# Whole weight tiles for the last three pairs, eight chunks with outputs of their own, other planner constants, and a last output tile in two halves

## The chip, the core and the metric

The kernel runs on one core of a Trainium2 chip. Its engines are TensorE (PE, with weight loads shown apart as PEld), VectorE (DVE), ScalarE (ACT), GpSimd (POOL) and SyncE (SP), which here only issues DMAs. The metric is the device time of one execution in microseconds, the median of several.

## The reference

A gated linear attention (a state of 48 by 48 per head that decays by alpha at each step) is followed by a feed-forward layer. 4 batches, 8 heads, 768 steps, head size 48; then 3072 tokens of width 384, hidden width 2048.

```python
state = alpha[t, :, None] * state + k[t] (outer) v[t]     # per batch and head
y[t] = q[t] @ state
h = x @ w_in                                              # x: y as [3072, 384]
g = where(h >= 1, h, where(h <= -1, 0, (h + 1) ** 2 / 4))
out = g @ w_out
```

## The kernel before

**Attention.** The steps are cut into 24 chunks of 128 steps, 6 for each batch. For a chunk, `prepare` loads alpha, k, q and v, makes running products of alpha on VectorE (two scans, lines 546 and 572) and scales q and k by them (lines 586 and 592). Chunks 0 to 6 (`EARLY`) arrive by step and are transposed on PE first (line 485), so that their scans read PSUM; later chunks arrive by head dimension and their scans read SBUF. `attend` then multiplies on PE: keys transposed (line 613), `scores` (628), `update` of the state (641) and `outputs` (768). For chunks below `MERGE` the output product follows in a PE operation of its own once the masks (714) are done; from the chunk after `MERGE` on, one PE operation (`burst`) does the update and scores of chunk j and the outputs of chunk j - 1. `end_chunk` splits the result into a high and a low part in fp32r (lines 792 on ACT, 797 on DVE) and puts it into `ring`.

**Feed-forward.** Chunks form 8 groups of 3 (384 tokens). For each group the 16 blocks f of the hidden width are taken in turn: `hidden` multiplies ring by w_in (line 864, 9 matmuls for the three products of high and low parts), then clips (DVE 908), squares (ACT 893), takes the larger (DVE 919), rounds to fp32r (ACT 923) and subtracts to get the low part (line 924, GpSimd; the very last on DVE). `second` multiplies the result gh by w_out (line 942, 9 matmuls) into three PSUM banks. Two banks hold hidden products, three buffers each hold gf and gh. Groups 0 and 1 share the first half of the weights, then the second half, with their partial sums parked in DRAM. After the last block of a group the three output tiles are copied from PSUM (ACT, or DVE where the planner finds it earlier) and sent out by SP (lines 988 to 1007).

**Weights.** They come as float64: 8 pairs u (blocks 2u and 2u + 1), each with a tile of w_in and one of w_out, 128 x 768 eight-byte words. `decode` turns a tile into a high and a low fp32r part: two ACT conversions (364, 372), two DVE bit operations (380, 391), an integer addition (404), an ACT rounding (417) and a subtraction (419). The addition and the subtraction run on GpSimd, or on DVE where the planner finds that earlier. `PIECES = 2` cuts each of these two into halves of 384 columns, for all pairs.

**The order.** All of it is written as operations with a cost in us, a key and their dependences (`plan.op`), and `Plan.order` simulates the engines in program build: on each engine it takes, among the operations that could begin soonest, the one of the lowest key, and the kernel emits its instructions in the resulting order. Keys count in blocks of the feed-forward. The key of a chunk is its due time, spread over the group before, less a margin (`MARGIN0` for group 0, `MARGIN1` for group 1, `MARGIN` for the rest); that of a weight pair's decode is the first block that needs it less `DECODE` (pair 0: `DECODE0`), and `LAG` more for w_out:

```python
due = since + (begin[n] - since) * (j - first[n] + 1) / groups[n] - (MARGIN, MARGIN0, MARGIN1)[n + 1 if n < 2 else 0]
ready = key - (DECODE if u else DECODE0)
```

Pairs 5, 6 and 7 are first needed at blocks 18, 20 and 22. Where an operation has a second engine (`other`), it stands there with a key higher by `LATER`. Operations marked `port` on DVE and GpSimd are planned one after the other, never at once. PSUM banks of the attention are limited to three at a time, for the first two chunks (`ROOM`) to `FIRST`. Where the plan leaves PE idle early on, it puts in filling matmuls (line 1013). After the plan come a few checks on the running products (lines 1043 to 1058) and the read of a flag (1062).

Of the kernel before, what the change touches and what calls it, by code (L numbers as in the profile page):

```python
# [37 lines left out]
MARGIN0 = 9.0  # L38
MARGIN1 = 6.0
FETCH0 = 18.0  # L40
DECODE0 = 4.0
AHEAD = 15.0
FIRST = 4
ROOM = 2
LATER = 4.0
MERGE = 6
WARMTH = 165.0
PIECES = 2
QHELP = 1
# [183 lines left out]
def gated_attention_ffn(ctx: ExitStack, tc: tile.TileContext, q, k, v, alpha, laid, out):  # L233
    nc = tc.nc
# [76 lines left out]
    with ExitStack() as main:  # L311
# [14 lines left out]
        def buf(where, name, shape, bufs, dtype=F32):  # L326
            plan.pool(name, bufs)
            return Buf(name, lambda: pools[where].tile(shape, dtype, name=name, bufs=bufs))
# [16 lines left out]
        def decode(u, which, raw, parts, key):  # L345

            n = NW * DM

            cols = [slice(i * n // PIECES, (i + 1) * n // PIECES) for i in range(PIECES)]
            part = lambda a: parts().rearrange(PARTS[which])[:, a * n : (a + 1) * n]  # L350
            w = raw
            data = lambda: raw()
            if wide:
# [49 lines left out]
                for c in cols:  # L403
                    add = lambda e, c=c: e.tensor_tensor(  # L404
                        out=bits()[:, c], in0=bits()[:, c], in1=word(I32, 0)[:, c], op=ALU.add
                    )
                    plan.op(
                        "POOL",
                        0.04 + 1.78 / PIECES,
                        key,  # L410
                        lambda add=add: add(nc.gpsimd),
                        [w, raw, (u, which)],
                        [w],
                        port=True,
                        other=("DVE", 0.2 + 1.4 / PIECES, lambda add=add: add(nc.vector), True),
                    )
            plan.op("ACT", 0.8, key, lambda: nc.scalar.copy(out=part(0), in_=data()), [w], [parts])  # L417
            for c in cols:
# [4 lines left out]
                    "POOL",  # L423
                    0.04 + 1.78 / PIECES,
                    key,
# [3 lines left out]
                    port=True,  # L429
                    other=("DVE", 0.08 + 0.8 / PIECES, lambda sub=sub: sub(nc.vector), True),  # L430
                )
# [419 lines left out]
        def hidden(n, f, key, c0=0, c1=GROUP):  # L851
# [73 lines left out]
            ends = (n, f) == (NG - 1, NF - 1)  # L925
            ways = [("POOL", 0.07 + 0.9 * w, lambda: sub(nc.gpsimd), True), ("DVE", 0.08 + 0.45 * w, lambda: sub(nc.vector), True)]
            (e, us, emit, port), other = reversed(ways) if ends else ways
# [5 lines left out]
        def second(seg, f, gh, key, c0=0, c1=GROUP):  # L933
# [30 lines left out]
            for t in ts:  # L964
                ps, ot = o_ps[seg][t], buf("fw", "ot", [P, DM], GROUP)
                place = ("sums", n, t)
                if f0 > 0:
# [274 lines left out]
```

## Time and profile before

| | us |
|---|---|
| median of 3 runs | 521.48 (521.29 to 549.84) |
| the profiled execution | 522.73 |
| its span, first to last instruction | 521.0 |
| PE, DVE, ACT, POOL busy | 502.7, 355.5, 262.3, 269.4 |
| mean granted clock of PE | 0.991 |

The span is what all rows below count from; the profiled execution's own time is 1.73 us more. A row of a timeline gives start and length, the engine, the line of the kernel, output and inputs with their shape, and in brackets how long the engine was idle before it and what released it.

### The profile page before, as it was taken

How to read it: one execution, taken by the hardware profiler on the slowest of the kernel's cores; microseconds unless marked ns; L12 is line 12 of the kernel's file. 1: busy time of each engine (PE TensorE's matmuls, PEld its weight loads, DVE VectorE, ACT ScalarE, POOL GpSimd, SP SyncE). 2: the span in 40 equal slices, each digit the busy share in tenths (PEclk: the TensorE clock that was granted, in tenths of full speed). 3: DMA queues.
4: the chain of work that ended last, by engine and by line, in shares of the span. 5: the costliest groups of instructions: out<-in, count | busy, mean ns of one | idle time of the engine just before them, and what ended most of it. 6: DMA issues, size and time to landing. Idle time of an engine off the chain costs nothing.

```text
span 521.0 us, 12291 instructions
## 1 busy us (share of the span) xinstructions
PE 502.7 (97%) x4874; PEld 484.3 (93%) x4874; DVE 355.5 (68%) x674; ACT 262.3 (50%) x506; POOL 269.4 (52%) x300
## 2 busy tenths in 40 slices
PE   8899899979899999999999999999999999999995
PEld 6788789969899999999999999999999999999995
DVE  6899999877877757578567767478467785343333
ACT  2789997564734444444444443444444444333331
POOL 3678898999954354354354244353354242333330
PEclk9999999998999999999999999999999999999998
DMA  8997968013034323133123422133102200100001
GB/s 239 357 317 235 318 212 311 11 58 120 23 120 122 111 77 80 57 82 123 55 62 79 122 62 77 53 88 123 57 21 59 67 2 8 18 23 23 0 1 50
DMA packets 27902, 52.46 MB, mean 101 GB/s; under 512 B 3808, under 2 KB 13504, under 8 KB 27840
## 3 DMA queue, kind: packets, MB, share of 16 engines
q1 hardware_dynamic: 27840, 51.62, 32.2%
q8 instruction: 40, 0.66, 0.6%
q14 instruction: 22, 0.18, 0.1%
HBM read 43.65 MB, written 5.90 MB: 95 GB/s over the span
## 4 chain that ended last, share of the span: by engine, by line
PE 74%; DVE 9%; DMA 7%; POOL 5%; issue 2%; ACT 1%; SPq 0%; DVEq 0%; POOLq 0%; ACTq 0%
PE ps L942 33%; PE ps L864 32%; DMA wt<-in_laid_w_out 5%; PE ps L768 4%; PE ps L641 2%; POOL wt L419 2%; PE ps L628 2%; POOL gh L924 2%; PE ps L613 1%; DVE w L391 1%; POOL w L404 1%; DVE w L380 1%; DMA raw<-in_laid_tok_q 1%; DVE gf L908 1%; DVE Q L546 1%
## 5 line engine op out<-in xcount | busy, mean ns | idle before, releaser
L942 PE MATMUL ps<-wt,gh 128*128 128x384 f32 x1152 | 226.7, 342 | 5.1 <-POOL gh L924 3.0
L924 POOL TENSOR_TENSOR gh<-gf,gh 128x384 fp32r<-128x384 f32 (+1 forms) x127 | 143.3, 1133 | 162.5 <-ACT gh L923 114.1
L864 PE MATMUL ps<-ring,wt 128*128 128x384 f32 (+1 forms) x1170 | 223.7, 338 | 0.0
L942 PEld LDWEIGHTS ps<-wt,gh 128*128 128x128 f32 x1152 | 202.0, 189 | 7.7 <-POOL gh L924 4.1
L864 PEld LDWEIGHTS ps<-ring,wt 128*128 128x128 f32 x1170 | 204.9, 189 | 0.7 <-DVE ring L797 0.2
L893 ACT ACTIVATE gf<-gf,half_b 128x384 f32<-128x384 f32 x122 | 74.6, 616 | 112.2 <-DVE gf L908 109.3
L908 DVE TENSOR_SCALAR gf<-ps 128x384 f32<-128x384 f32 x122 | 67.0, 552 | 72.4 <-PE ps L864 63.7
L919 DVE TENSOR_TENSOR gf<-gf,ps 128x384 f32<-128x384 f32 (+1 forms) x130 | 70.4, 543 | 50.0 <-ACT gf L893 49.4
L923 ACT CAST gh<-gf 128x384 fp32r<-128x384 f32 (+1 forms) x130 | 65.9, 508 | 71.8 <-DVE gf L919 66.1
L419 POOL TENSOR_TENSOR wt<-w,wt 128x384 fp32r<-128x384 f32 x32 | 39.2, 1245 | 3.4 <-ACT wt L417 3.2
L404 POOL TENSOR_TENSOR w<-w,wt 128x384 int32<-128x384 int32 x30 | 31.0, 1047 | 5.3 <-DVE w L391 2.4
L572 DVE TENSOR_TENSOR_SCAN inv<-raw,bwd 128x511 f32<-128x511 f32 x17 | 33.2, 1954 | 0.0
L546 DVE TENSOR_TENSOR_SCAN Q<-raw,fwd 128x512 f32<-128x512 f32 x17 | 24.0, 1413 | 7.3 <-PE ps L768 7.2
L768 PE MATMUL ps<-Q,both 128*64 128x64 f32 x372 | 26.9, 225 | 1.6 <-issue 1.6
L745 POOL TENSOR_TENSOR state<-state,last 128x192 f32<-128x192 f32 x20 | 12.0, 598 | 30.9 <-DVE state L670 30.9
L768 PEld LDWEIGHTS ps<-Q,both 128*64 128x64 f32 x372 | 23.6, 137 | 4.3 <-issue 2.5
L660 ACT COPY both<-state 48x192 f32<-48x192 f32 x66 | 23.1, 349 | 8.3 <-POOL state L745 6.6
L616 ACT COPY ks<-ps 128x512 f32<-128x512 f32 x24 | 14.1, 586 | 25.9 <-PE ps L613 25.9
L768 PE MATMUL ps<-other,both 128*64 128x64 f32 x372 | 26.7, 225 | 0.0
L592 POOL TENSOR_TENSOR Q<-Q,raw 128x512 f32<-128x512 f32 x18 | 24.1, 1337 | 3.4 <-DVE inv L564 2.0
L714 DVE TENSOR_TENSOR Q<-ps,mask 64x256 f32<-64x256 f32 x48 | 20.3, 423 | 7.5 <-ACT other L678 6.3
L768 PEld LDWEIGHTS ps<-other,both 128*64 128x64 f32 x372 | 23.5, 138 | 0.0
(78 smaller groups left out, 422.6 us busy)
## 6 DMA issues: line engine op xcount, KB each, us to landing
both<-in_laid_v_both SPq DMA_DIRECT2D x48, 128.0 KB, 3.0
wt<-in_laid_w_in SPq DMA_DIRECT2D x8, 768.0 KB, 7.5
wt<-in_laid_w_out SPq DMA_DIRECT2D x8, 768.0 KB, 8.1
vt<-in_laid_v SPq DMA_DIRECT2D x24, 192.0 KB, 2.9
out<-ot SPq DMA_DIRECT2D x24, 192.0 KB, 2.5
raw<-in_laid_dim_a SPq DMA_DIRECT2D x17, 256.0 KB, 2.9
raw<-in_laid_dim_k SPq DMA_DIRECT2D x17, 256.0 KB, 2.9
raw<-in_laid_dim_q SPq DMA_DIRECT2D x17, 256.0 KB, 2.6
```

Of the source, the lines that this page charges most:

```text
L404: add = lambda e, c=c: e.tensor_tensor(out=bits()[:, c], in0=bits()[:, c], in1=word(I32, 0)[:, c], op=ALU.add)
L419: sub = lambda e, c=c: e.tensor_tensor(out=part(1)[:, c], in0=data()[:, c], in1=part(0).bitcast(F32)[:, c], op=ALU.subtract)
L546: lambda: nc.vector.tensor_tensor_scan(flat(Q()), aT(), flat(fwd), 0.0, ALU.mult, ALU.max),
L572: lambda: nc.vector.tensor_tensor_scan(flat(inv())[:, 0:n][:, ::-1], aT()[:, 1 : n + 1][:, ::-1], flat(bwd)[:, 0:n][:, ::-1], bwd[:, G - 1 ...
L768: nc.tensor.matmul(out=ps()[halves[r], to, halves[u]], lhsT=lhsT[:, r, u], rhs=x()[:, g, halves[u]], start=m + u == 0, stop=True, skip_gro ...
L864: nc.tensor.matmul(out=h(), lhsT=win(f, w)[:, kt], rhs=ring[:, at, kt, a, :], start=(m == 0), stop=(m == 3 * KT - 1),)
L893: lambda: nc.scalar.activation(out=gf(), in_=in_(), func=func, scale=scale, bias=bias),
L908: lambda: nc.vector.tensor_scalar(out=gf(), in0=h(), scalar1=-1.0, scalar2=1.0, op0=ALU.max, op1=ALU.min),
L919: lambda: nc.vector.tensor_tensor(out=gf(), in0=gf(), in1=h(), op=ALU.max),
L923: plan.op("ACT", 0.08 + 0.41 * w, key + 0.4, lambda: nc.scalar.copy(out=gh()[:, 0], in_=gf()), [gf], [gh])
L924: sub = lambda e: e.tensor_tensor(out=gh()[:, 1], in0=gf(), in1=gh()[:, 0].bitcast(F32), op=ALU.subtract)
L942: nc.tensor.matmul(out=o_ps[seg][t](), lhsT=gh()[:, a, (t - c0) * CH : (t - c0 + 1) * CH], rhs=wout(f, w), start=(f == f0 and i == 0), sto ...
```

## The change

- `decode` cuts the addition and the subtraction into two only for pairs below `HALVES` = 5; pairs 5, 6 and 7 do each as one instruction of 768 columns. Their planned costs go from 0.93 (a half) to 1.015, and 1.83 for a whole one.
- The planned cost of line 924 on GpSimd goes from 0.97 to 1.00 for 384 columns.
- `MERGE` goes from 6 to 8: chunks 0 to 7 have their outputs in an operation of their own, and the first joined operation is that of chunk 9 with the outputs of chunk 8.
- `DECODE0` goes from 4 to 10, `MARGIN1` from 6 to 5, `FIRST` from 4 to 7.
- The last output tile is copied in two halves of 192 columns, one on ACT and one on DVE; ACT's half is sent from ACT's queue, DVE's from SP's.

```diff
-MARGIN1 = 6.0
+MARGIN1 = 5.0
-DECODE0 = 4.0
+DECODE0 = 10.0
-FIRST = 4
+FIRST = 7
-MERGE = 6
+MERGE = 8
-PIECES = 2
+HALVES = 5
...
-            cols = [slice(i * n // PIECES, (i + 1) * n // PIECES) for i in range(PIECES)]
+            pieces = 2 if u < HALVES else 1
+            cols = [slice(i * n // pieces, (i + 1) * n // pieces) for i in range(pieces)]
...
                         "POOL",
-                        0.04 + 1.78 / PIECES,
+                        0.2 + 1.63 / pieces,
...
-                        other=("DVE", 0.2 + 1.4 / PIECES, lambda add=add: add(nc.vector), True),
+                        other=("DVE", 0.2 + 1.4 / pieces, lambda add=add: add(nc.vector), True),
...
                     "POOL",
-                    0.04 + 1.78 / PIECES,
+                    0.2 + 1.63 / pieces,
...
-                    other=("DVE", 0.08 + 0.8 / PIECES, lambda sub=sub: sub(nc.vector), True),
+                    other=("DVE", 0.08 + 0.8 / pieces, lambda sub=sub: sub(nc.vector), True),
...
-            ways = [("POOL", 0.07 + 0.9 * w, lambda: sub(nc.gpsimd), True), ("DVE", 0.08 + 0.45 * w, lambda: sub(nc.vector), True)]
+            ways = [("POOL", 0.1 + 0.9 * w, lambda: sub(nc.gpsimd), True), ("DVE", 0.08 + 0.45 * w, lambda: sub(nc.vector), True)]
...
                 ps, ot = o_ps[seg][t], buf("fw", "ot", [P, DM], GROUP)
+                r0 = (first[n] + t) * CH
+                if seg == segs[-1] and f0 == 0 and t == ts[-1]:
+                    for e, copied, c in (("ACT", 0.3, slice(0, DM // 2)), ("DVE", 0.33, slice(DM // 2, DM))):
+                        o = plan.op(
+                            e, copied, key, lambda e=e, c=c, ps=ps, ot=ot: copy(e, ot()[:, c], ps()[:, c]), [ps], [ot],
+                            beside=e == "DVE",
+                        )
+                        q_ = {"ACT": ("ACT", nc.scalar), "DVE": ("SP", nc.sync)}[e]
+                        plan.op(
+                            q_[0],
+                            Plan.ISSUE,
+                            key + 1,
+                            lambda q_=q_, c=c, r0=r0, ot=ot: q_[1].dma_start(out=out[r0 : r0 + CH, c], in_=ot()[:, c]),
+                            [],
+                            [],
+                            moved=P * DM * 2,
+                            after=[o],
+                        )
+                    continue
```

## Rows read from the trace of the kernel before

**Rows 1.** The page: busy us, share of the span, instructions.
```profile
PE 502.7 (97%) x4874; PEld 484.3 (93%) x4874; DVE 355.5 (68%) x674; ACT 262.3 (50%) x506; POOL 269.4 (52%) x300
```
**Rows 2.** Windows: stretch, its length, busy us by engine, clock, DMA share, GB/s.
```profile
20.00:70.00 50.00, 45.44 (x658) 39.70 (x657) 47.71 (x95) 44.87 (x90) 42.24 (x54) 1.00 0.88 282
90.00:141.00 51.00, 46.02 (x413) 44.15 (x411) 39.69 (x61) 30.03 (x52) 50.66 (x44) 0.93 0.16 49
141.00:500.00 359.00, 359.00 (x3289) 352.14 (x3289) 228.38 (x446) 156.38 (x309) 147.16 (x163) 1.00 0.23 65
```
**Rows 3.** Timeline of PE around its idle time between 110 and 137 us.
```profile
112.27 0.61 PE L942 MATMUL ps<-wt,gh 128*128 128x384 f32 x2 [0.33 <-ACT gh L923]
115.88 2.61 PE L942 MATMUL ps<-wt,gh 128*128 128x384 f32 x7 [3.00 <-POOL gh L924]
...
136.60 1.66 PE L942 MATMUL ps<-wt,gh 128*128 128x384 f32 x8 [1.66 <-POOL wt L419]
```
**Rows 4.** Windows behind that idle time.
```profile
116.00:122.00 6.00, 6.00 (x19) 6.00 (x20) 5.94 (x8) 2.54 (x5) 5.83 (x5) 0.50 0.39 142
137.00:141.00 4.00, 4.00 (x108) 3.61 (x106) 3.18 (x8) 3.54 (x7) 4.00 (x5) 1.00 0.02 4
```
**Rows 5.** The chain that ended last: start, us, what (113 to 137 us).
```profile
113.86 1.01 POOL w L404
...
134.84 1.72 POOL wt L419
```
**Rows 6.** Timelines of ACT and of POOL ahead of the gap of 3 us.
```profile
111.70 0.51 ACT L923 CAST gh<-gf 128x384 fp32r<-128x384 f32 x1 [0.15 <-DVE gf L919]
...
110.35 3.55 POOL L419 TENSOR_TENSOR wt<-w,wt 128x384 fp32r<-128x384 f32 x2 [0.17 <-ACT wt L417]
...
114.83 0.99 POOL L924 TENSOR_TENSOR gh<-gf,gh 128x384 fp32r<-128x384 f32 x1
```
**Rows 7.** Single lines: durations in ns min/median/max; last row: busy us, mean ns.
```profile
L404 DVE CUSTOM_DVE_ANT_0 w<-wt,w x2: 880/893/906, 91.8 to 136.1; 128x768 uint16<-128x768 uint16 x2
...
L419 POOL TENSOR_TENSOR wt<-w,wt x32: 996/1026/1947, 24.1 to 140.7; 128x384 fp32r<-128x384 f32 x32
...
L924 POOL TENSOR_TENSOR gh<-gf,gh 128x128 fp32r<-128x128 f32 x1 | 0.5, 458 | 0.1
```
**Rows 8.** Groups of instructions between 90 and 141 us: busy us, mean ns, idle before.
```profile
L419 POOL TENSOR_TENSOR wt<-w,wt 128x384 fp32r<-128x384 f32 x16 | 22.0, 1396 | 0.2 <-ACT wt L417 0.2
L924 POOL TENSOR_TENSOR gh<-gf,gh 128x384 fp32r<-128x384 f32 x12 | 15.0, 1247 | 0.0
L919 DVE TENSOR_TENSOR gf<-gf,ps 128x384 f32<-128x384 f32 x13 | 7.1, 549 | 8.3 <-ACT gf L893 8.3
```
**Rows 9.** Timeline of PE: outputs of chunk 5 alone, and of chunk 6 joined.
```profile
63.58 0.30 PE L768 MATMUL ps<-Q,both 128*64 128x64 f32 x2 [0.26 <-issue]
...
101.15 0.27 PE L768 MATMUL ps<-Q,both 128*64 128x64 f32 x1
```
**Rows 10.** The end: chain, SP's issues, a window, landing (us), a half-width copy (ns).
```profile
515.28 0.56 DVE ot L340
...
515.34 1.02 SPq L1001 DMA_DIRECT2D out<-ot  x1
...
516.46 0.38 SPq L1001 DMA_DIRECT2D out<-ot  x1
...
517.00:518.00 1.00, 0.00 (x0) 0.00 (x0) 0.00 (x0) 0.00 (x0) 0.00 (x0) 0.96 0.93 342
...
out<-ot SPq DMA_DIRECT2D x24, 192.0 KB, 2.5
...
L668 DVE COPY state<-ps x4: 357/358/358, 14.0 to 334.4; 128x192 f32<-128x192 f32 x4
```
**Rows 11.** The second scan, from SBUF and from PSUM: ns min/median/max.
```profile
L572 DVE TENSOR_TENSOR_SCAN inv<-raw,bwd x17: 1336/2072/2660, 81.9 to 417.4; 128x511 f32<-128x511 f32 x17
L572 DVE TENSOR_TENSOR_SCAN inv<-ps,bwd x7: 1270/1272/1272, 7.2 to 67.2; 128x511 f32<-128x511 f32 x7
```

## The prediction

> **What bounds the kernel now.** I read the busy times first: TensorE (PE) is busy for 502.7 of 521.0 us, VectorE 355.5, GpSimd 269.4 [rows 1]. A share of the whole span hides stages, so the table by stage comes next [rows 2]. From 141 to 500 us PE is busy 359.00 of 359.00 us at full clock: a step that only moves helper work there gives nothing. From 20 to 70 us VectorE is the fullest engine (47.71 of 50, ScalarE 44.87). From 90 to 141 us it is GpSimd: 50.66 of 51, while PE has 46.02 and a granted clock of 0.93. PE is idle for 4.6 us from 20 to 70, 5.0 us from 90 to 141 and 5.8 us at the end, after its last product, whose copy begins at 515.28 [rows 10].
>
> The timeline of PE shows where the 5.0 us lie [rows 3]: 0.33 us and 3.00 us inside one second product at 112.27 us, released by the GpSimd subtraction that makes the low half of gh (line 924), and 1.66 us at 136.60 us, released by line 419, the last step of a weight tile's decode. The 3 us gap has a second price. From 116 to 122 us the granted clock reads 0.50, the lower of the two levels (1.2 GHz) [rows 4], so those 6.1 us of products are worth half: about 3.1 us more. The 1.66 us gap has no such tail: the clock is 1.00 from 137 us on. Together PE loses 3.33 + 3.1 + 1.66 = 8.1 us between 112 and 137 us.
>
> The chain of waits says who sets this: from 113.86 to 136.56 us it is mostly GpSimd, lines 404, 924 and 419 in turn, and then PE [rows 5]. GpSimd's own timeline shows the gap being made [rows 6]: two halves of line 419 take 3.55 us, a half of line 404 another 1.01, and only then, at 114.83, comes the gh that PE has waited for since 112.9 and whose input ScalarE had ready at 112.2. So between 90 and 137 us PE can only come sooner if GpSimd has less to do, or waits less.
>
> **The change part by part.** *Whole tiles for pairs 5, 6 and 7 (HALVES).* Three pairs have six tiles; each has two steps cut in two now, so 24 half instructions become 12 whole ones. No whole one is in the trace. GpSimd's subtraction of 128 columns took 458 ns and an undisturbed half of 384 takes 996 [rows 7]: (996 - 458) / 256 = 2.10 ns a column and 0.19 us fixed. A whole tile of 768 columns is then 0.19 + 1.61 = 1.80 us against 1.99: 0.19 us saved twelve times, 2.2 us. The other part is waiting. Between 90 and 141 us line 419 has a mean of 1396 ns against 996 at best, so each half waits some 0.4 us [rows 8]; a pair of halves can wait twice, a whole instruction once. For six subtractions that is up to 6 x 0.4 = 2.4 us; I take 0.8, since a longer instruction is also met by more VectorE instructions. A step that the planner gives to VectorE instead takes 1.80 us off GpSimd (two halves went there, 893 ns each [rows 7]); VectorE has 11.3 us free from 90 to 141 [rows 2]. I count none of it, and keep two such steps, 3.6 us, for the low end. Value: -3.0 us; ends: 0 (PE's wait moves to another place) and -2.2 - 2.4 - 3.6 = -8.2, which is as much as PE loses there. The last two whole instructions (pair 7, second tile) come after 136.6 us and count for little; that is inside the rounding of the 0.8.
>
> *Eight chunks end at once (MERGE 6 to 8).* Chunks 6 and 7 get their own output product instead of one joined to the next chunk's scores. Nothing is added but the joins: where chunk 5 does this now, PE waits 0.26 us ahead of the output matmuls; in the joined form (chunk 7's scores with chunk 6's outputs) no gap is shown ahead of them [rows 9]. For two chunks that is 0.5 us; chunk 7's falls into the stretch where PE has idle time anyway, so +0.3. Ends 0 and +1. The evictions of both chunks (lines 792 and 797) come one chunk earlier; they are ScalarE and VectorE work, not GpSimd's.
>
> *Order (DECODE0, FIRST, MARGIN1 and the new costs).* None of these adds an instruction. DECODE0 lets the first weight pair go ahead of chunk 2's work, MARGIN1 puts chunks 3 to 5 one block later against the products of group 0, FIRST lets chunks 0 and 1 hold seven PSUM banks. The DMA issues keep their keys except those of chunks 3 to 5, which SP may pass behind a weight load. What can be won up to 70 us is what the fullest engine leaves: VectorE's 2.29 us [rows 2]; what can be lost has no row, so I take the stall already seen as its size, 3.3 us. Value: -0.7 (a third of the 2.29). The raised costs (a half from 0.93 to 1.015 us, line 924 from 0.97 to 1.00) agree with 996 ns at best, and with 0.99 us, in the trace [rows 6, 7]; they make the planned order truer but shorten nothing.
>
> *The last output tile in halves.* Now VectorE copies three tiles; the last copy begins at 515.28 and takes 0.56 us [rows 10], while SP is still in the second issue (1.02 us, the third 0.38) and issues the third only at 516.46. After it some 4.2 us pass to the end of the span. A copy of half the columns took 358 ns [rows 10], so the halves are ready 0.2 us earlier; ScalarE's goes out beside SP, VectorE's still stands behind SP's second issue if that keeps its 1.02 us. Half a tile is 96 KB; at the 342 GB/s of the last full microsecond [rows 10] it is 0.29 us shorter than a whole one. Value -0.5; ends +0.4 (the new queue costs one issue of 0.38 and saves nothing) and -1.2 (SP's second issue takes 0.38 as well). Behind the new issue on ScalarE nothing is queued but the read of the flag.
> The Trainium skill (DMA: Bandwidth & Descriptors, Anatomy of one DMA — SWDGE (gpsimd) path) speaks against much gain here: nearly all of a small transfer is a fixed time of about 2.0 us, mostly the receipt of the last byte, and only bytes / 436 GB/s scales. By it the halving gives 0.23 us, and this term would be -0.2 instead of -0.5. The landings of whole output tiles, 2.5 us at the median for 192 KB [rows 10], agree with that rule.
>
> **Sum.** -3.0 + 0.3 - 0.7 - 0.5 = -3.9 us. The profiled execution took 522.73 us, its span of 521.0 and 1.73 around it; it is 1.25 us over the median of the runs, 521.48. 522.73 - 3.9 = 518.8 for it, 521.48 - 3.9 = 517.6 for the median.
>
> **The rivals.**
> *A. The whole tiles stand in gh's way (slower).* A gh that comes just behind a whole instruction waits up to 1.80 us instead of 1.00 on GpSimd's queue. PE runs two hidden products ahead at most, then stops; a gap of 3 us like the one at 112 us brings the clock down and costs 3.33 + 3.1 = 6.4 us in all. It decides from the point where a new gap is as long as that one; one of 1.66 us costs only itself. For it: GpSimd is full, and that gh already waited 2.6 us there [rows 6]. Against it: the planner knows the longer cost and can put gh first. One more gap of this kind, the other terms as before without the gain of 3.0: 521.48 + 6.4 - 0.9 = 527.0.
> VectorE scans that read SBUF take 2072 ns at the median against 1272 from PSUM, while the VectorE step of gh at line 919, which reads gf and PSUM, keeps a mean of 549 [rows 8, 11]. The Trainium skill (SBUF — State Buffer, Who interferes with whom) names this a lock: GpSimd or a VectorE instruction with two SBUF inputs holds the shared port pair for its whole length. The rows agree, and by it whole instructions hold VectorE up longer: this belongs to A.
> *B. All of it comes back.* Truer costs, shorter work and a step or two on VectorE close both gaps, and the clock stays up: -8.1 - 0.7 - 0.5 + 0.3 = -9.0, 512.5; with the early idle time gone too (-2.3 instead of -0.7) 510.9, which is past 2%. For it: VectorE's free 11.3 us. Against: GpSimd must lose 8 us of 51, and the arithmetic above finds 3.
> *C. Hidden anyway.* The gap moves from 112 to 137 us and keeps its size, since what GpSimd saves goes into waits for VectorE; only the tail is left: 521.48 - 0.5 + 0.3 = 521.3. For it: line 419's 0.4 us and line 924's 0.26 us (1247 ns against 0.99 us) of waiting per instruction depend on the order, and the order is new throughout.
>
> **How the numbers follow.** My forecast 0.42, A 0.18, B 0.18 (a third of it past 2%), C 0.22. What a measurement of this kernel can tell from no change is about 2%, 10.4 us: faster means under 511.1, slower over 531.9. Faster 0.07 from B; slower 0.04 from A with two such gaps (533); the rest, 0.89, is within 2%. The range reaches from 511.5, which leaves out only B's far end, to 526.5, just short of A's 527.0, since A has smaller gaps too. The forecast's own range is 515 to 520.
>
> **What would show it.** Right: lines 404 and 419 appear 12 times fewer in all, with 768-column forms near 1.8 us on GpSimd; PE's idle time from 90 to 141 us falls by some 3 us, and the chain there still runs through GpSimd; the stages after 141 us keep PE at 100%; two shorter copies at the end and a last landing some 0.5 us earlier. Wrong: whole instructions above 2.5 us at the mean, a new PE gap of 3 us released by line 924 with a clock of 0.50 behind it (A); no PE gap over 1 us and no stretch below full clock after 90 us (B); or an early stretch in which PE idles more than the 4.6 us of 20 to 70.

## The result, and the profile after

The change made the kernel slower: 525.94 us (median of 5 runs) against 521.92 us for the kernel before, a ratio of 1.0069 with an interval of 1.0043 to 1.0096. That is 3.6 us (0.0069 of 521.5) on the other side of the forecast of -3.9. The profiled execution took 525.63 us, its span 523.9, which is 2.9 us more than the span before. One of the five runs of the kernel before took 549.84 us, in a slower state of the chip; all ratios here are of fast runs.

Below, a ratio is always to the kernel before, run on the same chip; "us by ratio" is the ratio less 1, times 521.5. Where two variants are compared, it is the difference of their ratios.

The windows of the kernel after (stretch, its length, busy us of PE, PEld, DVE, ACT and POOL, clock, DMA share, GB/s) come first, as they did before.

```profile
0.00:20.00 20.00, 18.30 (x274) 15.42 (x275) 15.19 (x34) 10.13 (x22) 9.50 (x23) 1.00 0.92 306
20.00:70.00 50.00, 43.46 (x643) 39.15 (x642) 47.41 (x90) 46.85 (x94) 39.86 (x51) 1.00 0.82 281
70.00:90.00 20.00, 17.42 (x171) 16.46 (x170) 18.14 (x28) 14.76 (x26) 14.45 (x15) 0.91 0.82 262
90.00:141.00 51.00, 47.19 (x339) 45.01 (x338) 44.72 (x63) 28.14 (x50) 48.01 (x33) 0.97 0.20 63
141.00:500.00 359.00, 358.22 (x3338) 350.84 (x3338) 227.50 (x446) 156.31 (x310) 147.53 (x165) 1.00 0.23 64
```

Two windows of the kernel before complete [rows 2].

```profile
0.00:20.00 20.00, 17.05 (x264) 14.06 (x265) 13.99 (x29) 9.01 (x18) 8.09 (x21) 1.00 0.91 294
70.00:90.00 20.00, 20.00 (x173) 19.70 (x173) 18.78 (x34) 17.51 (x32) 17.20 (x17) 1.00 0.86 296
```

Go down the column of PE. Its idle time falls by 1.25 us up to 20 us, grows by 1.98 from 20 to 70, by 2.58 from 70 to 90, falls by 1.17 from 90 to 141 and grows by 0.78 behind that: +2.9 us. The clock costs, as an estimate from these rows, some 1.6 us from 70 to 90 (17.42 busy us at 0.91) where it cost nothing, and some 1.4 from 90 to 141 (47.19 at 0.97) where it cost some 3.2 (46.02 at 0.93): -0.2. With a tail that is 0.13 us shorter, this makes +2.6 of the span's +2.9. So the stretch that the prediction worked on did get better. A new stall stands ahead of it, and the early stretch idles more.

The timeline of PE in the kernel after shows the new waits of these two stretches, and the longest one behind them.

```profile
79.67 0.33 PE L769 MATMUL ps<-Q,both 128*64 128x64 f32 x2 [1.79 <-DVE Q L715]
80.67 0.24 PE L769 MATMUL ps<-other,both 128*64 128x64 f32 x1 [0.67 <-DVE other L715]
111.77 0.30 PE L769 MATMUL ps<-Q,both 128*64 128x64 f32 x2 [2.59 <-issue]
132.60 1.49 PE L943 MATMUL ps<-wt,gh 128*128 128x384 f32 x7 [0.79 <-POOL gh L925]
```

Line 769 is the output product (768 before). The first two rows are chunk 6, the third is chunk 7: the two chunks that `MERGE` 8 gave an output product of their own. The gaps of 3.00 and 1.66 us of the kernel before [rows 3] are gone; the longest wait for gh is 0.79 us.

What chunk 6's outputs waited for is on VectorE. First its timeline, then GpSimd's at the same time.

```profile
73.60 5.17 DVE L547 TENSOR_TENSOR_SCAN Q<-raw,fwd 128x512 f32<-128x512 f32 x1
...
79.20 0.88 DVE L715 TENSOR_TENSOR Q<-ps,mask 64x256 f32<-64x256 f32 x2
```

```profile
73.73 1.01 POOL L925 TENSOR_TENSOR gh<-gf,gh 128x384 fp32r<-128x384 f32 x1
74.71 1.99 POOL L420 TENSOR_TENSOR wt<-w,wt 128x384 fp32r<-128x384 f32 x2
76.67 1.02 POOL L925 TENSOR_TENSOR gh<-gf,gh 128x384 fp32r<-128x384 f32 x1
```

The masks of chunk 6 (line 715) stand in VectorE's queue behind the first scan of chunk 7, the first chunk whose scans read SBUF. That scan took 5.17 us. In the kernel before, the scan at this place took 1.35. From 73.73 to 77.69 us four GpSimd instructions run without a break and at their usual length, and the scan ends 1.1 us after the last of them.

Chunk 7's outputs waited for something else. ScalarE's timeline, then VectorE's:

```profile
109.30 0.83 ACT L418 CAST wt<-w 128x768 fp32r<-128x768 f32 x1 [4.78 <-POOL w L405]
110.16 0.62 ACT L679 COPY other<-Q 64x512 f32<-64x512 f32 x1
```

```profile
110.80 0.86 DVE L715 TENSOR_TENSOR Q<-ps,mask 64x256 f32<-64x256 f32 x2 [1.58 <-ACT other L679]
```

ScalarE waits 4.78 us for a weight tile's addition on GpSimd. Behind it in the queue stands a copy for chunk 7 (line 679) that doesn't need that tile, and VectorE's masks wait for the copy. The granted clock behind this gap is below 1 for a while: 0.97 from 90 to 141 us.

The whole tiles, in GpSimd's groups by shape (x count, busy us, mean ns, idle time ahead and its releasers):

```profile
L420 POOL TENSOR_TENSOR wt<-w,wt 128x384 fp32r<-128x384 f32 x20 | 19.8, 1008 | 1.4 <-ACT wt L418 1.1
L420 POOL TENSOR_TENSOR wt<-w,wt 128x768 fp32r<-128x768 f32 x6 | 12.0, 1996 | 0.1
...
L405 POOL TENSOR_TENSOR w<-w,wt 128x768 int32<-128x768 int32 x4 | 8.4, 2099 | 2.4 <-issue 1.5 <-DVE w L392 0.9
```

Ten whole instructions are on GpSimd (two went to VectorE), at a mean of 1996 and 2099 ns; the halves of line 420 now have a mean of 1008. The means mix instructions that were held up with others that were not. One of the latter:

```profile
113.50 1.83 POOL L420 TENSOR_TENSOR wt<-w,wt 128x768 fp32r<-128x768 f32 x1
```

The shortest whole instructions take 1.83 to 1.89 us, against 1.99 for two undisturbed halves [rows 7]; the longest take 2.55 and 2.80 us.

### The profile page after: what moved, and what is told of

Read it like the earlier page. It is cut to its first block, busy times and chain, and to the rows that moved or that the text cites. A ratio compares the mean times of both kernels' runs of the same rounds, so it can differ in the third digit from the quotient of the medians.

```text
span 523.9 us, 12246 instructions
## 1 busy us (share of the span) xinstructions
PE 502.9 (96%) x4861; PEld 484.4 (92%) x4861; DVE 360.8 (69%) x674; ACT 262.2 (50%) x507; POOL 264.4 (50%) x288
## 4 chain that ended last, share of the span: by engine, by line
PE 76%; DVE 11%; POOL 5%; issue 4%; ACT 3%; DVEq 0%; POOLq 0%
PE ps L943 33%; PE ps L865 32%; PE ps L769 4%; DVE Q L547 2%; PE ps L642 2%; POOL gh L925 2%; PE ps L629 2%; POOL w L405 2%; PE ps L614 2%; DVE w L381 1%; DVE inv L573 1%; DVE Q L715 1%; POOL wt L420 1%; ACT gf L894 1%; DVE w L392 1%
## 5 line engine op out<-in xcount | busy, mean ns | idle before, releaser
L925 POOL TENSOR_TENSOR gh<-gf,gh 128x384 fp32r<-128x384 f32 (+1 forms) x129 | 146.7, 1141 | 167.3 <-ACT gh L924 118.4
L405 POOL TENSOR_TENSOR w<-w,wt 128x384 int32<-128x384 int32 (+1 forms) x24 | 31.5, 1326 | 8.1 <-DVE w L392 5.5
L769 PE MATMUL ps<-Q,both 128*64 128x64 f32 x372 | 28.6, 229 | 5.8 <-issue 4.0
L547 DVE TENSOR_TENSOR_SCAN Q<-raw,fwd 128x512 f32<-128x512 f32 x17 | 27.7, 1630 | 7.4 <-PE ps L769 7.2
L420 POOL TENSOR_TENSOR wt<-w,wt 128x384 fp32r<-128x384 f32 (+1 forms) x26 | 31.8, 1236 | 1.4 <-ACT wt L418 1.1
L769 PE MATMUL ps<-other,both 128*64 128x64 f32 x372 | 28.2, 229 | 1.2 <-DVE other L715 0.8
```

The costliest lines, as they stand in the source:

```text
L405: add = lambda e, c=c: e.tensor_tensor(out=bits()[:, c], in0=bits()[:, c], in1=word(I32, 0)[:, c], op=ALU.add)
L420: sub = lambda e, c=c: e.tensor_tensor(out=part(1)[:, c], in0=data()[:, c], in1=part(0).bitcast(F32)[:, c], op=ALU.subtract)
L547: lambda: nc.vector.tensor_tensor_scan(flat(Q()), aT(), flat(fwd), 0.0, ALU.mult, ALU.max),
L769: nc.tensor.matmul(out=ps()[halves[r], to, halves[u]], lhsT=lhsT[:, r, u], rhs=x()[:, g, halves[u]], start=m + u == 0, stop=True, skip_gro ...
L925: sub = lambda e: e.tensor_tensor(out=gh()[:, 1], in0=gf(), in1=gh()[:, 0].bitcast(F32), op=ALU.subtract)
```

## The experiments

| kernel | what it is | us | ratio to before | interval |
|---|---|---|---|---|
| after | the change | 525.94 | 1.0069 | 1.0043 to 1.0096 |
| a_merge6 | after, MERGE 6 | 521.41 | 0.9995 | 0.9977 to 1.0013 |
| a_halves8 | after, all tiles in halves | 524.71 | 1.0065 | 1.0047 to 1.0083 |
| a_costs | after, old planned costs | 523.59 | 1.0041 | 1.0024 to 1.0057 |
| a_consts | after, old constants | 530.09 | 1.0174 | 1.0151 to 1.0198 |
| b_merge8 | before, MERGE 8 | 523.90 | 1.0032 | 1.0012 to 1.0051 |
| b_halves | before, whole tiles and new costs | 527.49 | 1.0101 | 1.0069 to 1.0134 |
| b_costs | before, new costs | 525.34 | 1.0082 | 1.0065 to 1.0099 |
| b_consts | before, new constants | 520.73 | 0.9979 | 0.9958 to 1.0001 |
| b_jit | before, planned cost of a half on GpSimd 0.01 us higher | 525.74 | 1.0088 | 1.0066 to 1.0110 |
| f_whole | before, its order kept, whole tiles | 523.23 | 1.0031 | 1.0010 to 1.0052 |
| f_later | after, outputs 6 and 7 later on PE | 529.34 | 1.0149 | 1.0115 to 1.0184 |
| f_scan | after, one GpSimd instruction moved | 523.10 | 1.0030 | 1.0015 to 1.0045 |
| f_act | f_scan, one ScalarE instruction moved | 522.51 | 1.0018 | 0.9996 to 1.0040 |
| f_scan_m6 | f_scan with MERGE 6 | 518.81 | 0.9955 | 0.9940 to 0.9970 |
| f_scan_m6_h8 | f_scan_m6, all tiles in halves | 521.90 | 1.0012 | 0.9989 to 1.0035 |
| b_tail_act | before, another split tail | 521.34 | one run | |

A kernel whose name begins with a_ or b_ is planned anew, so its order changes along with the edit (in b_tail_act only at the end, by its expectation). One that begins with f_ keeps the order of the kernel that it is made from, but for what is said (f_scan_m6 that of a_merge6); f_scan_m6_h8 alone among them is planned anew, with the same move in it.

### MERGE, alone and undone

```diff
-MERGE = 8
+MERGE = 6
```

> The changed kernel with MERGE back at 6 and all else kept. Theory 1 (the output products of chunks 6 and 7, now in operations of their own, make PE wait for masks that are late): both waits ahead of line 769 in the changed kernel (1.79 + 0.67 us at 80 us, 2.59 + 0.17 us at 112 us) and the two stretches of lower clock behind them (0.83 for 10 us each, 3.4 us together) go, so up to 8.6 us less: 517 to 521 us, with no wait over 1 us ahead of line 769 after 70 us. Theory 2 (the new order up to 70 us) and theory 3 (whole tiles): 525 to 527 us, since neither is touched.

> The kernel before with MERGE 8 and nothing else. Theory 1: waits ahead of line 768 for chunks 6 and 7 appear, 525 to 530 us. Theories 2 and 3: within 1.5 us of 521.9.

Undone in after, MERGE 8 gives back 0.0074, or 3.9 us by ratio, and the output product's waits go with it. Alone in before, it costs 1.7 us (523.90, in neither expected range), in another way: the waits ahead of the output products are small (0.42 us at 111 us), but second products wait for gh, as one of five such rows of b_merge8 shows:

```profile
127.93 1.50 PE L942 MATMUL ps<-wt,gh 128*128 128x384 f32 x7 [1.39 <-POOL gh L924]
```

So the edit costs in both places, and what it costs depends on where the planner then puts it. The slow scan is still there in a_merge6 (first row, VectorE), but now a second product pays for it (PE, then the windows):

```profile
73.22 5.17 DVE L547 TENSOR_TENSOR_SCAN Q<-raw,fwd 128x512 f32<-128x512 f32 x1
```

```profile
84.21 0.61 PE L943 MATMUL ps<-wt,gh 128*128 128x384 f32 x2 [1.99 <-ACT gh L924]
85.42 1.98 PE L943 MATMUL ps<-wt,gh 128*128 128x384 f32 x7 [0.59 <-DVE gf L920]
```

```profile
70.00:90.00 20.00, 17.41 (x146) 16.47 (x145) 17.58 (x30) 14.11 (x24) 13.92 (x16) 0.91 0.81 271
90.00:141.00 51.00, 47.93 (x437) 45.53 (x436) 45.26 (x66) 30.93 (x54) 47.90 (x35) 1.00 0.18 56
```

From 70 to 90 us PE loses as much without MERGE 8 as with it: 2.59 us idle for 2.58, at the same clock of 0.91. So this stall belongs to the scan and not to MERGE 8, and the low clock there did not go, though theory 1 said that it would. Most of what MERGE 8 costs lies behind 90 us: up to 141 us PE of a_merge6 is busy for 47.93 us at full clock, in after for 47.19 at 0.97, and from 141 to 500 us after idles 0.78 us and a_merge6 not at all. That is some 3 us of the 3.9, as an estimate.

### The scan beside GpSimd's row

In f_scan all queues are those of after but for one instruction. The small GpSimd operation that reads the scan's result (`last`, line 556) goes ahead of three GpSimd instructions, two halves of line 420 and one of line 925, so that GpSimd has to wait for the scan.

```diff
...
+            order.remove(lasts[7])
+            order.insert(order.index(scans[7]) + 1, lasts[7])
...
```

> The changed kernel in its own order, only one small GpSimd instruction of chunk 7 (line 556, which reads the result of the scan of line 547) ahead of three others in GpSimd's queue, so that GpSimd waits for that scan. In the changed kernel the scan began at 73.60 us and took 5.17 us beside four GpSimd instructions in a row; its median is 1.28. Theory 6 (VectorE was kept from the shared read path by GpSimd's row and that made the gap and the low clock at 80 us): the scan takes under 2.5 us, PE waits less than 1 us at 80 us, the clock there stays at 1.00, and the time falls by 3 to 5 us to about 522. If not theory 6: scan still over 4 us, time within 1 us of 525.9.

VectorE's timeline of f_scan, and GpSimd's (lines are one higher than in after):

```profile
73.86 2.22 DVE L548 TENSOR_TENSOR_SCAN Q<-raw,fwd 128x512 f32<-128x512 f32 x1
```

```profile
73.98 1.02 POOL L926 TENSOR_TENSOR gh<-gf,gh 128x384 fp32r<-128x384 f32 x1
76.16 0.22 POOL L557 TENSOR_SCALAR last<-Q 128x4 f32<-128x4 f32 x1 [1.17 <-DVE Q L548]
76.47 2.00 POOL L420 TENSOR_TENSOR wt<-w,wt 128x384 fp32r<-128x384 f32 x2
```

```profile
70.00:90.00 20.00, 20.00 (x197) 19.34 (x196) 17.84 (x32) 15.62 (x28) 17.09 (x17) 1.00 0.87 287
```

The scan takes 2.22 us, about one GpSimd instruction (1.02) more than the 1.28 of an undisturbed one; against four instructions in a row (3.96 us) it took 3.9 more. GpSimd idles 1.17 us, and PE's loss in this stretch is gone: from 70 to 90 us it is busy without a gap at full clock, as the last row shows. This settles the gap at 80 us. The time falls by 0.0039, 2.0 us by ratio and not the 3 to 5 of the expectation, though the stretch won some 4.2 (2.58 idle and some 1.6 of clock). The rest went behind 90 us: chunk 7's outputs wait longer (PE's row), and the clock behind them is lower than in after (the window).

```profile
109.11 0.45 PE L770 MATMUL ps<-Q,both 128*64 128x64 f32 x2 [3.23 <-issue]
```

```profile
90.00:141.00 51.00, 46.44 (x387) 43.92 (x386) 46.10 (x66) 29.93 (x52) 47.95 (x33) 0.93 0.19 59
```

The same one-instruction move with MERGE 6:

> The kernel after with MERGE 6 (521.4 us), and in it only GpSimd's `last` of chunk 7 moved ahead of the two halves of a weight tile, as was worth 2.8 us with MERGE 8. Theory: the scan beside GpSimd's row costs here too; the scan falls from 5.17 to under 2 us, the gaps of 1.99 and 0.59 us at 84 us and the low clock behind them go, and the time is 518 to 519, under both kernels. Rival: without outputs standing behind the scan it is hidden: the scan is shorter, the gaps stay, and the time is 521.4.

It won 0.0040, 2.1 us, here too, and this kernel is faster than both: 518.81 us, 2.4 us under before by ratio. The four kernels make a table of ratios:

| | MERGE 8 | MERGE 6 |
|---|---|---|
| scan beside GpSimd's row | 1.0069 (after) | 0.9995 (a_merge6) |
| scan ahead of it | 1.0030 (f_scan) | 0.9955 (f_scan_m6) |

Down either column the scan's place is worth 2.0 or 2.1 us, and along either row MERGE 8 costs 3.9. The two losses are apart from each other, and without both the rest of the change wins 2.4 us. Neither MERGE 8 nor the whole tiles bring the slow scan: it takes 5.17 us in a_merge6 and 5.16 in a_halves8. The new costs and the new constants bring it together. With either undone it is gone, as VectorE's rows of a_costs and of a_consts show (both further down):

```profile
76.14 1.86 DVE L547 TENSOR_TENSOR_SCAN Q<-raw,fwd 128x512 f32<-128x512 f32 x1
```

```profile
79.66 1.35 DVE L547 TENSOR_TENSOR_SCAN Q<-raw,fwd 128x512 f32<-128x512 f32 x1
```

### The gap of chunk 7

> The changed kernel in its own order, only the output products of chunks 6 and 7 four operations later in PE's queue. Theory 1: the waits ahead of line 769 for these chunks (1.79 + 0.67 and 2.59 + 0.17 us) go or shrink under 1 us in all; if nothing else ends last, 5 to 8 us less than 525.9. If helpers are the limit all the same (theory 5), the idle time comes back further on ahead of line 943 and the time stays within 1.5 us of 525.9.

This run didn't test what it was made for. A chunk's v is loaded into `both[j % 2]` (line 519), two slices in all. Put four PE operations later, the outputs of chunks 6 and 7 came behind the loads of chunks 8 and 9 into the same slices. By the program's order they read those chunks' v: what this kernel leaves out is the outputs of chunks 6 and 7 with their own v. PE's row and SP's:

```profile
88.07 0.45 PE L770 MATMUL ps<-Q,both 128*64 128x64 f32 x2 [7.22 <-DMA both<-in_laid_v_both]
```

```profile
80.00 1.11 SPq L520 DMA_DIRECT2D both<-in_laid_v_both  x2
```

PE waited 7.22 us for a load of 7.8 us that should have followed these outputs. All it shows is how far the outputs can be put off: the next load of their slice bounds it. Whether a later place within that bound helps wasn't tried.

f_act instead moves what holds the masks. On top of f_scan, ScalarE's copy for chunk 7 goes ahead of the rounding that waits for GpSimd.

```diff
...
+            at = order.index(turns[7])
+            order.remove(turns[7])
+            at = max(i for i in range(at) if order[i].engine == "ACT")
...
+            order.insert(at, turns[7])
...
```

> The kernel with GpSimd's `last` of chunk 7 moved (523.1 us), and in it one more instruction moved: ScalarE's `other` copy of chunk 7 goes ahead of the rounding of a weight tile that stands before it and waits 4.8 us for GpSimd. Theory: ScalarE's order makes the second gap. The masks of chunk 7 then wait only for the state addition ahead of them on VectorE, the gap of 3.23 us at 109 us shrinks by the 1.57 us that VectorE idled, to about 1.7, and the time is 521 to 522. Rival: the gap is the outputs' place in PE's order alone (their masks stand behind a scan and the state in any case); then it stays above 3 us and the time is 523.

The output product of chunk 7 in f_act's PE, and the window:

```profile
107.07 0.30 PE L770 MATMUL ps<-Q,both 128*64 128x64 f32 x2 [1.72 <-issue]
```

```profile
90.00:141.00 51.00, 45.13 (x387) 41.41 (x386) 46.90 (x68) 29.99 (x53) 48.59 (x34) 1.00 0.20 64
```

The gap fell from 3.23 us to 1.72, by the 1.5 us that VectorE had idled: that link of the chain is shown. With the shorter gap the low clock behind it went as well: 1.00 from 90 to 141 us, where f_scan has 0.93. The two are worth some 4.5 us as an estimate (1.5, and 46.44 us at 0.93), yet the time moved by 0.6 us (522.51, not the expected 521 to 522), within the intervals. Most of it was given back some us later: PE now waits for gh at 113.89, 117.68, 124.87 and 129.07 us (1.17, 0.38, 0.64 and 0.80), while in f_scan between 110 and 141 us there is one such wait, of 0.55. So in this stretch, where GpSimd is busy for 48.59 of 51 us, a stall removed on another engine came back for the most part as waits for GpSimd. It also means that the wait of chunk 7's outputs alone doesn't carry the 3.9 us of MERGE 8; what carries the rest isn't shown.

### Whole tiles

f_whole keeps before's order on every engine and runs pairs of halves of pairs 5 to 7 as one instruction each, in the place of the first half. Its trace has ten such instructions, six of the subtraction and four of the addition (the expectation counts eleven).

```diff
...
+            if u < WHOLE or any(o.engine != "POOL" for o in ops):
+                do(nc.gpsimd)
+            elif i == 0:
+                do(nc.gpsimd, c=slice(0, NW * DM))
...
```

> The kernel before in its own order, every engine's queue as it was, with 11 pairs of half instructions of pairs 5, 6 and 7 on GpSimd put together to whole ones at the place of the first half. Theory 3 (whole instructions are in the way by their length): slower, 524 to 528, with a gap at 112 us longer than the 3.0 us of before. Theory 4 (they save what the rows said, 0.19 us each, and what made b_halves 5.6 us slower is the other order that the new costs bring): 518 to 522, whole instructions at 1.8 to 2.7 us.

```profile
112.57 0.62 PE L954 MATMUL ps<-wt,gh 128*128 128x384 f32 x2 [1.93 <-ACT gh L935]
115.29 2.61 PE L954 MATMUL ps<-wt,gh 128*128 128x384 f32 x7 [2.11 <-POOL gh L936]
135.33 1.66 PE L954 MATMUL ps<-wt,gh 128*128 128x384 f32 x8 [1.45 <-POOL wt L430]
```

GpSimd is busy 48.85 us from 90 to 141 instead of 50.66, so 1.8 us were saved on it. PE's three gaps are 5.5 us against 5.0 before [rows 3]: the stall moved and kept its size. The time is 1.6 us longer by ratio, 523.23, between the two expected ranges. The profiled execution, 521.41, is the fastest of the ten, so its rows need not show all of the loss. One thing that they do show is what holds the gh of the first gap up. GpSimd's row, VectorE's beside it, and VectorE's at this place in before:

```profile
108.78 1.85 POOL L430 TENSOR_TENSOR wt<-w,wt 128x768 fp32r<-128x768 f32 x1
```

```profile
108.84 2.61 DVE L399 SCALAR_TENSOR_TENSOR w<-wt,w 128x768 int32<-128x768 int32 x1
```

```profile
110.21 0.94 DVE L391 SCALAR_TENSOR_TENSOR w<-wt,w 128x768 int32<-128x768 int32 x1
```

VectorE's bit operation, 0.94 us in before, began 0.06 us after a whole subtraction of 1.85 and took 2.61. The next instruction on VectorE makes gf for this gh. In before the bit operation began first, and it was GpSimd's two halves that took longer (3.55 us for 1.99 [rows 6, 7]).

Undone in after, with the order planned anew, whole tiles are worth nothing (0.2 us by ratio, with the waits ahead of line 769 still there):

```diff
-HALVES = 5
+HALVES = 8
```

> The changed kernel with HALVES 8, so that all pairs are in halves again and the new costs, order constants, MERGE 8 and tail stay. Theory 3: 521 to 523. Theory 1: 525 to 527, with the waits ahead of line 769 still there.

And in the best version halves cost 3.0 us by ratio, more than either expectation, again in another order, with waits of 1.54 and 1.84 us for gh at 110 and 128 us:

> The kernel with MERGE 6 and `last` of chunk 7 moved (518.8 us), with all tiles in halves (HALVES 8). Theory: whole tiles save GpSimd 0.19 us an instruction, some 2 us, in the stretch that GpSimd bounds; in halves it is 520.5 to 521. Rival: what they save goes into waits; 518.5 to 519.

### The order by itself

> The kernel before with whole tiles for pairs 5, 6 and 7 and the new costs, nothing else. My forecast for this part was -3.0 us, 518.9. Theory 3 (whole instructions on GpSimd are in the way): 525 to 527. Theory 1: 516 to 521, the 3 us gap at 112 us and the 1.7 us gap at 136 us smaller or gone.

> The kernel before with DECODE0 10, MARGIN1 5 and FIRST 7, nothing else. Theory 2: slower by about the 3.6 us of the whole change, 525 to 526, with PE idle for 6 us or more from 20 to 70 us (4.6 before). Theory 1: 520 to 523.

```diff
-                        0.04 + 1.78 / PIECES,
+                        0.2 + 1.63 / PIECES,
...
-            ways = [("POOL", 0.07 + 0.9 * w, lambda: sub(nc.gpsimd), True), ("DVE", 0.08 + 0.45 * w, lambda: sub(nc.vector), True)]
+            ways = [("POOL", 0.1 + 0.9 * w, lambda: sub(nc.gpsimd), True), ("DVE", 0.08 + 0.45 * w, lambda: sub(nc.vector), True)]
```

> The kernel before with the new planned costs alone: 1.015 for 0.93 us (a half of the addition or subtraction) and 1.00 for 0.97 us (line 924 of before); all tiles stay in halves, no instruction is added, only the order changes. Theory: the loss of 5.6 us with whole tiles for three pairs came from the new order that costs bring, not from the whole instructions; this kernel then is slower too, 524 to 527. Rival: truer costs are harmless and the whole instructions cost it: 521 to 522.

b_halves cost 5.3 us by ratio, and the constants alone gained 1.1, which their interval doesn't part from nothing. The costs alone, with every tile in halves, cost 4.3, so most of b_halves' loss can come without a whole tile. The next kernel asks how much a number that means nothing is worth:

```diff
-                        0.04 + 1.78 / PIECES,
+                        0.05 + 1.78 / PIECES,
```

> The kernel before with the planned cost of a half on GpSimd at 0.94 us for 0.93: no instruction added or removed, but the planner's ties fall otherwise and the order changes from about 30 us on. Theory: the order that a change of numbers draws is worth several us by itself; this kernel then differs from before by more than 1 us, to either side (with b_costs at +4.1 I expect slower, 523 to 525). Rival: only a change of some size matters, and it is 521 to 522 as before.

It cost 4.6 us by ratio. The longest of its new waits on PE:

```profile
63.98 1.23 PE L485 MATMUL ps<-ident,raw 128*128 128x128 f32 x8 [2.80 <-issue]
```

Its instructions are those of before but for the planner's filling matmuls and its choices between two engines. A planned cost that differs by 0.01 us is enough for another order. Costs and constants undone in after:

> The kernel after (525.9 us) with the planned costs of before (0.93 us for a half, 1.82 for a whole tile, 0.97 for line 925); MERGE 8, whole tiles, constants and tail stay. Theory: the costs alone made before 4.1 us slower by another order, so taking them back wins 3 to 4 us: 522 to 523. Rival: the loss belongs to MERGE 8, whose outputs wait for their masks under any costs: 525 to 526, with waits over 1 us ahead of the output products again.

> The kernel after with MARGIN1 6, DECODE0 4 and FIRST 4 as before. In before the new ones won 1.1 us. Theory: they help by giving chunks 0 to 5 room early and do so here too; without them 526.5 to 528. Rival: their worth is an accident of one order; then it is as likely under 525.

The old costs give 1.5 us back by ratio, between the two expectations and not clear of the intervals. The slow scan is gone in a_costs, but chunk 7's outputs still wait 2.52 us for their masks at 109 us, as the rival said. The old constants cost 5.5 us more, with one wait of 3.14 us at 133 us for a weight tile (line 420). What an edit is worth changes by several us from one order to the next: MERGE 8 costs 1.7 or 3.9 us, the costs 4.3 or 1.5, the constants gain 1.1 or 5.5, and whole tiles lie between a loss of 1.6 and a gain of 3.0.

PE's idle time from 20 to 70 us grew by 2.0 us, from 4.6 to 6.5, and this too comes from costs and constants together. It is 6.2 us in a_merge6 and a_halves8, which have both, and 3.9 to 4.9 in a_costs, a_consts, b_costs and b_consts, which have one of them (a_costs and b_costs with a clock of 0.97 and 0.93 there).

### The tail

The tail of the kernel after: ScalarE, VectorE, SP and PE, one after the other.

```profile
518.71 0.32 ACT L340 COPY ot<-ps 128x192 f32<-128x192 f32 x1 [3.08 <-DVE ot L340]
```

```profile
517.27 1.40 DVE L340 COPY ot<-ps 128x384 f32<-128x384 f32 x3 [1.05 <-PE ps L943]
```

```profile
517.86 1.40 SPq L1022 DMA_DIRECT2D out<-ot  x2
519.36 0.38 SPq L980 DMA_DIRECT2D out<-ot  x1
```

```profile
515.68 2.60 PE L943 MATMUL ps<-wt,gh 128*128 128x384 f32 x14
```

PE ends at 518.28, the span at 523.9: 5.62 us, against 5.75 before. VectorE's three copies end at 518.67, and ScalarE's half begins 0.04 us later, so the halves ran one after the other. VectorE's half, ready at 518.67, was sent at 519.36, behind SP's second issue (0.88 us). A half tile did not land sooner than a whole one (2.5 us [rows 10]), as the issues of both halves show:

```profile
out<-ot ACTq DMA_DIRECT2D x1, 96.0 KB, 2.4
out<-ot SPq DMA_DIRECT2D x1, 96.0 KB, 3.0
```

> The kernel before with the last output tile in halves, ScalarE's half into a buffer of its own and both halves sent from ScalarE's queue; all else in the same order. After had 5.62 us from PE's last product to the end of the span, before 5.75. Theory: the halves there ran one after the other because they share a tile, and the last one was sent behind SP's second issue; here both copies begin together, within 0.1 us, and the end comes 0.3 us earlier, 5.2 to 5.4 us after PE's last product. Rival: ScalarE starts later than VectorE in any case, or the second issue on its queue takes as long as SP's: 5.6 to 5.8.

ScalarE and VectorE of b_tail_act (PE ends at 514.12, the span at 519.6; the second issue on ScalarE's queue took 0.46 us):

```profile
514.54 0.32 ACT L340 COPY raw<-ps 128x192 f32<-128x192 f32 x1 [3.08 <-DVE ot L340]
```

```profile
513.11 1.40 DVE L340 COPY ot<-ps 128x384 f32<-128x384 f32 x3 [1.06 <-PE ps L942]
```

With a buffer of its own ScalarE's half still begins 0.03 us after VectorE's ends, so the shared tile was not the reason. Both halves read the same PSUM bank; banks apart weren't tried. The tail is 5.5 us, 0.1 less than in after and between the two expectations, in a single run.

## Why the prediction was wrong

**What bounds the kernel: right.** Everything happened ahead of 150 us; from there to 500 us PE is busy 350.00 of 350.00 us in before, after, f_scan and f_scan_m6 alike. GpSimd was rightly taken as the limit from 90 us on: in f_act a stall removed there came back for the most part as waits for gh. One reading was off and changes nothing: the 0.33 us at 112.27 us were released by ScalarE's rounding and not by GpSimd [rows 3].

**"Nothing is added but the joins" (+0.3, end at +1): the step that failed most.** The row of chunk 5's outputs with 0.26 us [rows 9] was taken as the price for chunks 6 and 7. MERGE 8 cost 3.9 us in after's order and 1.7 in before's. The forecast asked what the output product adds on PE, and not what is queued ahead of its masks. Chunk 6's masks stand on VectorE behind a scan, those of chunk 7 behind a ScalarE copy that itself stands behind a rounding waiting for GpSimd. Chunk 7's outputs waited 2.59 us in after and 3.23, 2.52, 1.29 and 0.98 in f_scan, a_costs, a_consts and a_halves8, and in a_merge6 there is no such wait. How much of the 3.9 us goes by this wait stays open: f_act took 1.5 us of it away and the time fell by 0.6, within the intervals, and a new order alone can be worth as much (4.6 us in b_jit).

**Order (-0.7): the second step that failed; the sign was a guess.** "What can be lost has no row" was true. The new costs and constants together put VectorE's scan of chunk 7 beside four GpSimd instructions in a row, and it took 5.17 us for 1.28. PE then idled 2.58 us from 70 to 90 us, with the clock at 0.91: 2.0 us of time, shown in two kernels by the place of one instruction. The early stretch idled 6.5 us instead of 4.6, the prediction's own last sign of being wrong. The rows that hint at the scan were at hand: the second scan's 2072 ns from SBUF [rows 11], and VectorE as the fullest engine of the early stretch [rows 2]. The 3.3 us taken as the size of a loss was the right magnitude for a bad order (b_jit 4.6, b_costs 4.3), but it was used as an end of the range and not as a likely case: in before four of the five edits that plan anew (b_merge8, b_costs, b_jit, b_halves) lost 1.7 to 5.3 us, and b_consts gained 1.1. That before's order is better than its neighbours because it was picked among many is likely, but not shown. The single edits don't add: b_costs 4.3, f_whole 1.6, b_merge8 1.7 and b_consts -1.1 make 6.5, and the whole change cost 3.6.

**Whole tiles (-3.0): right on GpSimd, wrong on PE.** The count is right: GpSimd ran 288 instructions for 300, in forms of 768 columns. The length is nearly right: the shortest whole instructions took 1.83 to 1.89 us for the forecast's 1.80, so each saves 0.10 to 0.16 us and not 0.19. What failed is that GpSimd's saving was counted as PE's. In f_whole 1.8 us were saved on GpSimd, PE's gaps kept their size, and the time grew by 1.6 us. That is what rival C said.

**Tail (-0.5): 0.13 measured.** The condition that the step named ("if that keeps its 1.02") held, with 0.88 us for SP's second issue, and the halves ran in turn. The 0.29 us for half the bytes didn't show: the halves landed 2.4 and 3.0 us after their issue. The Trainium skill's fixed time (DMA: Bandwidth & Descriptors, Anatomy of one DMA — SWDGE (gpsimd) path) gave an estimate of -0.2, nearer as a number. But that section is on DMAs that GpSimd issues, these are SP's and ScalarE's, and the 0.23 us that it leaves for half the bytes didn't show either.

**The rivals.** A's figure, 527.0, is near the result by luck. Its mechanism is not what happened: no wait for gh over 0.79 us is in the kernel after, and no low clock from one. Its side remark, that GpSimd holds VectorE up where both read SBUF, is what made the scan slow, in after with halves and in f_whole with a whole tile. B's signs (no gap over 1 us after 90 us) failed at 111.77 us. Without MERGE 8 and with the scan ahead (f_scan_m6), the rest of the change wins 2.4 us, where the forecast had 4.2 for it. The range, 511.5 to 526.5, held the result only just, and on the wrong side of no change.

**What stays open:** what carries the 3.9 us of MERGE 8 beside the wait of chunk 7's outputs, and why ScalarE's half waits for VectorE's in the tail.

## What to carry to other kernels

When an edit feeds a planner, price the order first: change a number that means nothing (here 0.01 us in one cost, +4.6 us; several such changes would give a spread) and take what it moves as the least uncertainty of any forecast; then test the edit itself with the old order written out. Where an operation gets a place of its own, look at what is queued ahead of its inputs on their engines, not at what it adds to its own. When the plan is settled, go through the few stalls left by hand: one small instruction that makes GpSimd wait for a scan was worth 2 us in two kernels, and gave the version that beat both.

## What the runs showed that was not expected

A VectorE scan reading SBUF can be held through a whole row of GpSimd instructions, not just one: 5.17 us beside four in a row (3.96 us), 2.22 beside one (1.02), with GpSimd at its usual pace in both. It can also go the other way: in the kernel before the scan at this place took 1.35 us, and the two halves of line 419 beside it 2.93 instead of 2.00. VectorE's row there, and GpSimd's:

```profile
77.69 1.35 DVE L546 TENSOR_TENSOR_SCAN Q<-raw,fwd 128x512 f32<-128x512 f32 x1
```

```profile
77.91 2.93 POOL L419 TENSOR_TENSOR wt<-w,wt 128x384 fp32r<-128x384 f32 x2
```

The Trainium skill (SBUF — State Buffer, Who interferes with whom) calls the port pair that VectorE and GpSimd share an exclusive lock: of VectorE's two-port modes it says that whoever issues first gets the pair for the whole instruction while the other blocks, and a VectorE instruction with two SBUF inputs, like this scan, it lists as one that contends with GpSimd's reads. The one-instruction delay agrees. Whether a blocked scan gets its turn between two GpSimd instructions went both ways: in after it did not for four in a row, while in f_whole a scan (line 558) that began at 111.84 us beside a whole tile ended after it, in 2.62 us, and the next GpSimd instruction took 1.92 us. What decides this is open.
